# Attention, Fourier mixing and a two-layer network on one core: norm statistics spread over engines, two-part queries and keys in quarter-array form, eleven plain tiles

## The chip, the cores and the metric

One core of one Trainium2 chip. The metric is device time in microseconds of one execution, the median over several runs. The engines are TensorE (PE; its weight loads are listed as PEld), VectorE (DVE), ScalarE (ACT), GpSimd (POOL) and SyncE (SP), which here issues nearly all DMA transfers from one queue.

## The reference, cut to what matters

```python
# q, k, v: (8, 8, 576, 64); window of 64 keys, causal
scores = q @ k.T / 8; scores = where(0 <= pos_q - pos_k < 64, scores, -1e9)
attn = exp(scores - max); attn = attn / (sum(attn) + 1e-9)
x = (attn @ v) as (8, 576, 512)
mixed = real(fft(fft(x, axis=1), axis=2))
u = x + mixed
un = (u - mean(u)) / sqrt(var(u) + 1e-6)        # over the 512 features
out = u + relu(un @ w1) @ w2                     # w1: 512 x 2048, w2: 2048 x 512
```

All in float32. Most products are made in two 16-bit parts, high and low: a float32 value is split as hi = f16(x), lo = f16(x - hi), and a product needs three passes (hi hi, hi lo, lo hi; the list `PASSES`).

## The kernel before, in words

The 8 x 576 rows are 36 tiles of 128 rows. A tile T of a pair of batches goes through `attn_tile`; nine tiles are a pair. After tiles 4 and 8 of a pair the Fourier block `fft` of one batch follows, and then `norm_tile` for the four or five tiles that are complete. Two tiles make a chunk of 256 rows for the two layers: `ffn(0)` in float32 ("plain"), `ffn` of chunks 1 to 13 in two parts, `ffn7` of chunks 14 to 17 with a scheme of seven products. The weights come as 32 pieces of 512 KB, converted on VectorE in three steps (`weight_piece`), squared on ScalarE for their size, and split into two parts once all are there.

**Attention.** Tiles 0 to 12 (`whole`, T < PRO = 13) are plain: queries, keys and the weights of attention are turned with TensorE transposes in float32, and the score uses quarters of the array, 64 rows by 64 columns (L662). From tile 13 on all is in two parts: keys and queries are split (ScalarE or VectorE for the high, GpSimd or VectorE for the low part), turned with DMA transposes, one for the keys and two for the queries, which are laid out doubled (`qpad`, `qbd`). The keys stand as 128 rows, 64 of high and 64 of low parts, so that one matmul of 128 rows makes two of the three passes (L667); the score of a tile is two operations, one for the even and one for the odd heads (`score((g,))`). Behind the score come the mask with the row maximum (VectorE), the exponential (ScalarE), the turning of the weights, the product with the values (`av`, L746), and `normed` on VectorE: add 1e-9 to the sum, reciprocal, multiply (L752 to L758). Then a radix-4 step, whose result is turned on TensorE if `soon` (plain tiles, and tiles 4 and 8 of a pair), else by transfer.

**Norm.** `norm_tile`: for tiles from 2 on a gather (GpSimd's queue) brings the mixed rows; `stats` on VectorE adds them to x, takes `bn_stats` and `bn_aggr` and adds 1e-6 (L1092 to L1105); `rstd` on GpSimd raises to the power -0.5 (L1109); `scale` on VectorE makes un (L1113). Then un is split and turned for the chunk.

**Order.** Every piece of work is an `op` with an engine, or two to choose from (`alt`). The order in which all ops of all engines are issued is a list of numbers in the file (`ORDER`), and `SECOND` holds those that go to their second engine. `Plan.follow` walks the list; where its own arithmetic sees a gap on TensorE of over 0.8 us before the first layer begins, the kernel puts filler matmuls (`warm`, L1625). Each engine does its instructions in the order of the list; an op waits for its inputs by semaphores. All loads, transposes and stores stand in SP's queue in the order of the list.

Of the kernel before, what the change touches and what calls it, by code (L numbers as in the profile page):

```python
# [12 lines left out]
F32 = mybir.dt.float32  # L13
F16 = mybir.dt.float16
# [4 lines left out]
AF = mybir.ActivationFunctionType  # L19
# [27 lines left out]
PRO = 13  # L47
# [3 lines left out]
WSC = 1.1  # L51
W_DMA, W_DMA_STEP, W_CONV, W_SQ, W_SPLIT, W_STEP = -20, 1.6, 40, 60, 60, 0.5
VS = 64.0
YS = 32.0
# [138 lines left out]
""".split()}  # L193


# [1461 lines left out]
```

## Time and profile before

| | |
|---|---|
| median of 3 runs | 962.61 us (962.05 to 963.97) |
| span of the profiled execution | 961.9 us |
| outside the span, against the median | 0.7 us (no other time of that execution is given) |
| TensorE busy | 941.0 us, 98% |
| VectorE, ScalarE, GpSimd busy | 748.8, 413.2, 326.8 us |
| mean granted clock of TensorE | 0.995 |

A busy TensorE includes matmuls that overlap each other and filler; its time is best read from the starts of successive groups. Rows below are named Rows 1 to Rows 9. "L667" is line 667 of the kernel, "psc" the score's tile, "pa" the product with the values, "ph" and "po" the first and second layer's, "pk", "pq", "pp", "py" the results of transposes.

### The profile page before, as it was taken

What the parts mean: (1) busy time and instruction counts of PE and PEld (TensorE: products, weight loads), DVE (VectorE), ACT (ScalarE), POOL (GpSimd) and SP (SyncE); (2) the same over time, 40 slices, a digit from 0 to 9 for tenths busy, and PEclk for the clock granted to TensorE, in tenths of its full rate; (3) what the DMA queues carried; (4) which work ended last, traced back from release to release, by engine and by line L of the source; (5) the groups of instructions that cost most, each with busy time, mean ns of one, the idle gap of its engine ahead of it and who ended that gap; (6) DMA issues with size and microseconds to landing.
All of it is one profiled execution on the core that took longest, in us unless ns stands there. A gap on an engine that the chain in (4) does not pass through costs nothing.

```text
span 961.9 us, 23560 instructions
## 1 busy us (share of the span) xinstructions
PE 941.0 (98%) x9251; PEld 700.8 (73%) x9251; DVE 748.8 (78%) x2038; ACT 413.2 (43%) x929; POOL 326.8 (34%) x616
## 2 busy tenths in 40 slices
PE   7899999999999999999999999999999999999998
PEld 5677677676776676667676677667676668888887
DVE  6899788887887778786766877786887999686654
ACT  7775667734633344333533235333443334222231
POOL 1543333134643342413421424223333422241231
PEclk9999999999999999999999999999999999999999
DMA  9886735336797748697768665676765301121000
GB/s 220 228 253 188 214 88 136 75 92 127 137 206 175 158 93 166 154 176 149 139 140 170 127 127 97 153 139 154 118 151 91 81 13 34 38 54 46 23 33 23
DMA packets 307294, 119.93 MB, mean 125 GB/s; under 512 B 290728, under 2 KB 291112, under 8 KB 307184
## 3 DMA queue, kind: packets, MB, share of 16 engines
q1 hardware_dynamic: 304320, 109.40, 52.9%
q0 software_dynamic: 2720, 8.92, 3.6%
q8 instruction: 72, 1.18, 0.5%
q14 instruction: 38, 0.31, 0.1%
q10 hardware_dynamic: 144, 0.13, 0.0%
HBM read 54.99 MB, written 14.17 MB: 72 GB/s over the span
## 4 chain that ended last, share of the span: by engine, by line
PE 84%; DVE 8%; DMA 4%; issue 1%; POOL 1%; ACT 1%; SPq 0%; DVEq 0%; POOLq 0%; ACTq 0%
PE ph L1297 27%; PE po L1278 27%; PE ph L1451 9%; PE po L1426 7%; PE pa L746 3%; PE pz L1011 3%; PE pg L977 2%; PE psc L667 2%; DMA kn<-in_k 1%; DVE td L1371 1%; PE pp L703 1%; DMA kst<-flex 1%; PE py L837 1%; PE psc L662 1%; PE warm L1625 1%
## 5 line engine op out<-in xcount | busy, mean ns | idle before, releaser
L1278 PE MATMUL po<-w1s,hh 128*128 128x512 f16 (+1 forms) x1312 | 332.0, 390 | 1.4 <-DVE xu L1332 1.4
L1297 PE MATMUL ph<-uhl,w0s 128*128 128x256 f16 (+1 forms) x2616 | 330.6, 278 | 2.0 <-DVE hh L1309 1.7
L1297 PEld LDWEIGHTS <-w0s 128*128 128x128 f16 x2496 | 242.7, 98 | 62.9 <-issue 3.5
L1278 PEld LDWEIGHTS <-hh 128*128 128x128 f16 x1248 | 119.7, 98 | 106.9 <-issue 1.6
L1306 ACT ACTIVATE hh<-ph 128x512 f16<-128x512 f32 x104 | 61.9, 596 | 185.9 <-PE ph L1297 135.5
L692 ACT ACTIVATE pr<-pr,nm 128x128 f32<-128x128 f32 x288 | 91.3, 391 | 25.3 <-DVE nm L684 25.1
L1309 DVE SCALAR_TENSOR_TENSOR hh<-ph,hh 128x512 f16<-128x512 f32 x104 | 71.3, 685 | 30.1 <-ACT hh L1306 29.6
L1451 PE MATMUL ph<-uhl,w0s 128*128 128x256 f16 x768 | 90.6, 273 | 0.0
L1451 PEld LDWEIGHTS <-w0s 128*128 128x128 f16 x768 | 75.1, 98 | 9.6
L496 POOL TENSOR_TENSOR flex<-pr,flex 128x128 f16<-128x128 f32 x72 | 36.6, 539 | 111.8 <-ACT flex L486 67.7
L1085 POOL DMA_INDIRECT mt<-md,gix x34 | 36.2, 1065 | 104.3 <-DVE xu L1100 44.9
L684 DVE CUSTOM_DVE_ANT_0 pr<-psc,mskb 128x128 f32<-128x128 f32 x288 | 65.0, 284 | 8.0 <-PE psc L667 5.9
L1109 POOL TENSOR_TENSOR rs<-mv,mhalf 128x1 f32<-128x1 f32 x36 | 25.5, 709 | 104.4 <-DVE mv L1105 104.1
L496 POOL TENSOR_TENSOR up<-un,up 128x128 f16<-128x128 f32 x64 | 32.1, 531 | 53.7 <-ACT up L486 37.6
L1467 DVE TENSOR_TENSOR hx<-hx 128x128 f32<-128x128 f32 x100 | 26.1, 304 | 29.5 <-ACT hx L1462 28.7
L1462 ACT ACTIVATE hx<-ph 128x512 f32<-128x512 f32 x31 | 18.3, 597 | 71.5 <-PE ph L1451 62.3
L1426 PEld LDWEIGHTS <-hh 128*128 128x128 f16 x434 | 42.4, 98 | 4.8
L746 PE MATMUL pa<-ve,pt 128*64 128x65 f16 (+1 forms) x760 | 41.2, 205 | 2.8 <-ACT pt L486 1.3
L746 PE MATMUL pa<-va,pt 128*64 128x65 f16 (+1 forms) x760 | 41.3, 205 | 0.0
L496 POOL TENSOR_TENSOR flex<-kn,flex 128x128 f16<-128x128 f32 x52 | 27.0, 550 | 30.9 <-ACT flex L486 30.9
L1475 DVE TENSOR_TENSOR hl<-hx,hh 128x896 f16<-128x896 f32 x27 | 29.6, 1106 | 9.0 <-ACT hh L486 8.3
L496 POOL TENSOR_TENSOR flex<-qn,flex 128x128 f16<-128x128 f32 x72 | 32.0, 479 | 9.1 <-ACT flex L486 8.9
(221 smaller groups left out, 1610.2 us busy)
## 6 DMA issues: line engine op xcount, KB each, us to landing
wd<-in_moe_w_ch SPq DMA_DIRECT2D x20, 512.0 KB, 5.1
out<-xu SPq DMA_DIRECT2D x35, 256.0 KB, 2.7
kn<-in_k SPq DMA_DIRECT2D x32, 256.0 KB, 3.8
qn<-in_q SPq DMA_DIRECT2D x32, 256.0 KB, 4.2
flex<-in_moe_w_ch SPq DMA_DIRECT2D x12, 512.0 KB, 3.4
ve<-va SPq DMA_DIRECT2D x43, 130.0 KB, 2.5
flex<-in_v SPq DMA_DIRECT2D x20, 256.0 KB, 3.6
md<-mp SPq DMA_DIRECT2D x24, 192.0 KB, 2.3
```

Source lines behind the costliest of these rows:

```text
L496: eng.tensor_tensor(out=out[:, k : k + w], in0=in0[:, k : k + w], in1=in1[:, k : k + w], op=al)
L684: nc.vector.tensor_tensor_reduce(out=t["pr", g][:, hp], in0=t["ps", g][:, hp], in1=mskb[:, m : m + P], scale=-0.125, scalar=3.0e38, op0=AL ...
L692: nc.scalar.activation(pr, pr, AF.Exp, bias=t["nm", g][:, hp : hp + 1], scale=-1.0)
L746: nc.tensor.matmul(pa[sl, hp], pt[:, sl], v_, start=(x == 0), stop=(x == len(mm) - 1))
L1085: nc.gpsimd.indirect_dma_start(out=mts[T], out_offset=None, in_=mds[pb][0 : HR if n < 4 else 2 * HR], in_offset=bass.IndirectOffsetOnAxis( ...
L1278: nc.tensor.matmul(t["po"][i], l_, r_, start=(f == 0 and x == 0), stop=(f == NKF - 1 and x == len(mm) - 1))
L1297: nc.tensor.matmul(ph, l_, r_, start=(x == 0), stop=(x == len(mm) - 1))
L1306: nc.scalar.activation(t["hh", j][:, 0], ph, AF.Relu)
L1309: nc.vector.scalar_tensor_tensor(out=hh[:, 1], in0=ph, scalar=0.0, in1=hh[:, 0], op0=ALU.max, op1=ALU.subtract)
L1426: nc.tensor.matmul(t["po", bk][:, x], t["h", j][a][:, slot], right(n, j, b_), start=(j == 0 and k == 0 and n in opens), stop=(j == seven - ...
L1451: nc.tensor.matmul(ph, l_, r_, start=(x == 0), stop=(x == len(mm) - 1))
L1475: eng.tensor_tensor(out=lo[:, a:b_], in0=x[:, a + 1 : b_ + 1], in1=hi[:, a:b_], op=ALU.subtract)
```

## The change

Constants: PRO 13 to 11 (tiles 11 and 12 are done in two parts), new `PSC = 1.0`, `MEANS = 2`, `CEN = 512**-0.5`. ORDER and SECOND are new throughout (3201 ops instead of 3019). The order arithmetic no longer counts the small GpSimd steps (`port=None`) as sharing a port with VectorE.

Two-part keys and queries are both split into rows [high of all heads, low of all heads] and turned by one transfer each; the score is one operation for both halves of the heads, 3 passes x 16 matmuls of 64 rows by 64 columns. `normed` becomes three ops: `guard` (ScalarE or VectorE), `inverse` (a power on GpSimd or a reciprocal on VectorE), and the multiplication. In `norm_tile`, tiles 0 and 1 keep their statistics on VectorE; for the others the sum is made by the instruction that adds, the squares on ScalarE, the root on GpSimd, and the scaling on ScalarE or VectorE. The list SECOND sends to VectorE 34 of 72 guards, 29 of 72 inverses, and 10 of 34 scalings.

```diff
-PRO = 13
+PRO = 11
+MEANS = 2
...
-            op("ACT", 0.52, base, k_hi, [bk], [bkp], alt=("DVE", 0.34, lazy))
-            op("POOL", 1.12, base + 0.1, k_lo, [bk], [bkp], alt=("DVE", 0.6, lazy))
-            op("DMA", TURN, base + 0.2, k_turn, [bkp], [bkT], lat=2.0)
-            op("ACT", 0.95, base + 0.5, lambda e: q_part(0, e), [bq], Bfl[4:6], alt=("DVE", 0.6, lazy))
-            op("POOL", 2.1, base + 0.6, lambda e: q_part(1, e), [bq], Bfl[4:6], alt=("DVE", 1.13, lazy))
-            for j in range(2):
-                op("DMA", TURN, base + 0.7, lambda j=j: q_turn(j), Bfl[4:6], [Bq[i]], lat=2.8)
+            for nm, slot, dst, bsrc, bdst, lat, at in (
+                ("kn", 0, kst_, bk, bkT, 2.0, base), ("qn", 4 + i, q16[i], bq, Bq[i], 2.2, base + 0.5)
+            ):
...
+                op("ACT", 0.52, at, hi_, [bsrc], [Bfl[slot]], alt=("DVE", 0.34, lazy))
+                op("POOL", 1.12, at + 0.1, lo_, [bsrc], [Bfl[slot]], alt=("DVE", 0.6, lazy))
+                op("DMA", TURN, at + 0.2, turn_, [Bfl[slot]], [bdst], lat=lat)
...
             for hp in range(4):
-                for z in range(1 if whole else 2):
+                for x, (a, b_) in enumerate(mm):
                     for g in groups:
+                        rows = slice(64 * g, 64 * g + 64)
                         for jj in range(2):
...
+                            nc.tensor.matmul(
+                                t["ps", g][64 * jj : 64 * jj + 64, hp], qT[rows, 4 * a + hp, 64 * jj : 64 * jj + 64],
+                                keys(4 * b_ + hp, jj, rows), start=(x == 0), stop=(x == len(mm) - 1),
+                            )
...
-            op("DVE", 0.75, base + 6.2 + 0.5 * g, normed, [bpa], [bx], port=False)
+            op("ACT", 0.1, base + 6.05 + 0.5 * g, guard, [bpa, Bmh], [brc], alt=("DVE", 0.05, 0.0), port=False)
+            op("POOL", 0.54, base + 6.1 + 0.5 * g, inverse, [Bmh], [brc], alt=("DVE", 0.08, 0.0), port=None)
+            op("DVE", 0.42, base + 6.2 + 0.5 * g, normed, [bpa, brc], [bx], port=False)
...
-            bst_ = sm.tile([P, 6], F32, tag="st", name=f"st{T}")
-            nc.vector.bn_stats(out=bst_, in_=xt)
-            t["mv"] = sm.tile([P, 2], F32, tag="mv", name=f"mv{T}")
-            nc.vector.bn_aggr(out=t["mv"], in_=bst_)
-            nc.vector.tensor_scalar(out=t["mv"][:, 1:2], in0=t["mv"][:, 1:2], scalar1=1e-6, scalar2=None, op0=ALU.add)
+                nc.vector.tensor_tensor_reduce(
+                    out=xs, in0=xs, in1=ms, scale=1.0, scalar=0.0, op0=ALU.add, op1=ALU.add, accum_out=t["sm"][sl]
+                )
...
+        def spread():
+            t["un"] = sb([P, DM], F32, "un", f"un{T}")
+            nc.scalar.activation(
+                t["un"], xts[T], AF.Square, bias=t["mv"][:, 0:1], scale=CEN, accum_out=t["mv"][:, 1:2]
+            )
...
+            nc.gpsimd.tensor_scalar(out=t["rs"], in0=t["mv"][:, 1:2], scalar1=1e-6, scalar2=None, op0=ALU.add)
+            nc.gpsimd.tensor_tensor(out=t["rs"], in0=t["rs"], in1=mhalf, op=ALU.pow)
...
+            op("DVE", sum(0.95 if r else 0.8 for _, _, r in RANGES[n]), base + 0.5, stats, [bmt], [bx, bst])
+            op("ACT", 0.72, base + 0.55, spread, [bx, bst], [bun, bst])
+            op("POOL", 1.1, base + 0.6, rstd, [bst, Bmh], [brs], port=None)
+            op("DVE", 0.05, base + 0.65, shift, [brs, bst], [bnb])
+            op("ACT", 0.62, base + 0.7, scale, [bx, brs, bnb], [bun], alt=("DVE", 0.46))
```

## Rows read from the trace of the kernel before

**Rows 1.** The page, part 1: busy us (share of the span) xinstructions.
```profile
PE 941.0 (98%) x9251; PEld 700.8 (73%) x9251; DVE 748.8 (78%) x2038; ACT 413.2 (43%) x929; POOL 326.8 (34%) x616
```

**Rows 2.** Busy time by stretch: its us, PE busy, granted clock, DMA share, GB/s.
```profile
0.00:78.00 78.00, 65.39 (x839) 0.96 0.87 227
...
125.00:400.00 275.00, 275.00 (x2699) 1.00 0.64 132
400.00:600.00 200.00, 197.41 (x2012) 1.00 0.73 142
...
700.00:800.00 100.00, 98.51 (x884) 1.00 0.37 79
```

**Rows 3.** TensorE's waits: line <- releaser: us in total, times, longest us.
```profile
PE ph L1297 <- DVE hh L1309: 1.7, 3, 0.8
...
PE po L1278 <- DVE xu L1332: 1.4, 1, 1.4
```

**Rows 4.** The chain of waits, 0 to 80 us: start us, us, what.
```profile
45.62 0.45 PE pk L553 x4
46.09 5.55 DMA qn<-in_q
...
54.26 1.69 PE pg L977 x24
...
78.02 1.99 PE ph L1297 x8
```

**Rows 5.** The timeline of TensorE, 165 to 224 us: start us, us, group.
```profile
190.44 1.10 PE L662 MATMUL psc<-kst,qbd 64*64 64x128 f32 x32
...
199.92 0.60 PE L703 MATMUL pp<-ident,pr 128*128 128x128 f32 x4
200.36 1.46 PE L1278 MATMUL po<-w1s,hh 128*128 128x512 f16 x6
```

**Rows 6.** The timeline of TensorE, 191.4 to 192.3 us.
```profile
191.48 0.27 PE L746 MATMUL pa<-ve,pt 128*64 128x65 f32 x1
...
192.10 0.39 PE L1278 MATMUL po<-w1s,hh 128*128 128x512 f16 x1
```

**Rows 7.** The timeline of TensorE, 225 to 262 us.
```profile
230.59 1.47 PE L1297 MATMUL ph<-uhl,w0s 128*128 128x256 f16 x12
231.90 1.46 PE L1278 MATMUL po<-w1s,hh 128*128 128x512 f16 x6
233.20 1.47 PE L1297 MATMUL ph<-uhl,w0s 128*128 128x256 f16 x12
...
240.22 0.62 PE L667 MATMUL psc<-kst,qbd 128*64 128x128 f16 x16
240.67 0.19 PE L746 MATMUL pa<-ve,pt 128*64 128x65 f16 x1
...
241.04 0.61 PE L667 MATMUL psc<-kst,qbd 128*64 128x128 f16 x16
241.59 2.79 PE L1297 MATMUL ph<-uhl,w0s 128*128 128x256 f16 x24
...
252.24 1.46 PE L1278 MATMUL po<-w1s,hh 128*128 128x512 f16 x6
253.63 0.64 PE L667 MATMUL psc<-kst,qbd 128*64 128x128 f16 x16
```

**Rows 8.** The chain of waits over the whole span.
```profile
84.34 1.73 PE ph L1297 x8
```

**Rows 9.** Groups by line and shape: busy us, mean ns of one, idle before.
```profile
L1102 DVE BATCH_NORM_STATS2 st<-xu 128x6 f32<-128x512 f32 x36 | 25.0, 694 | 1.2
...
L1198 DVE SCALAR_TENSOR_TENSOR w0s<-wd,w0s 128x512 uint16<-128x512 uint32 x10 | 7.9, 787 | 0.0
...
L1204 ACT ACTIVATE junk<-w1s 128x512 f32<-128x512 f32 x16 | 10.0, 626 | 1.0 <-DVE w1s L1198 1.0
...
L1109 POOL TENSOR_TENSOR rs<-mv,mhalf 128x1 f32<-128x1 f32 x36 | 25.5, 709 | 104.4 <-DVE mv L1105 104.1
```

More of the change, by code (lines that the diff above doesn't have):

```diff
@@ L352, in follow @@
                 st = max(st, done[d.idx] + after + late * self.LATE[d.eng])
-            shared = e == "POOL" or e == "DVE" and o.port
+            shared = e == "POOL" and o.port is not None or e == "DVE" and o.port
             if shared:
@@ L409, in attn_fft_ffn_kernel @@
     mhalf = cp.tile([P, 1], F32, name="mhalf")
+    mone = cp.tile([P, 4], F32, name="mone")
+    eps = cp.tile([P, 2], F32, name="eps")
     mskb = cp.tile([P, 3 * P], BF16, name="mskb")
@@ L447, in attn_fft_ffn_kernel @@
     op("POOL", 0.3, -500, lambda: make_identity(nc, ident), writes=[Bid])
-    op("POOL", 0.1, -499, lambda: nc.gpsimd.memset(mhalf, -0.5), writes=[Bmh])
+    small = ((mhalf, -0.5), (mone, -1.0), (eps[:, 0:1], 1e-9), (eps[:, 1:2], VS * 1e-9))
+    op("POOL", 0.4, -499, lambda: [nc.gpsimd.memset(a_, v_) for a_, v_ in small], writes=[Bmh])
     op("POOL", 0.3, -300, lambda: nc.gpsimd.memset(unit, 1.0), writes=[Bones])
@@ L533, in attn_tile, with keys @@
         kst_ = (kst32 if whole else kst16)[:, T % 3 * kw : (T % 3 + 1) * kw].rearrange("p (h s) -> p h s", s=P)
-        def keys(h, jj, rows=slice(None)):
+        def keys(h, jj, rows):
             if jj or n == 0:
@@ L676, in attn_tile @@
             bpt.append([bt])
-            if not whole:
-                op("PE", 0.52, base + 2 + g, lambda g=g: score((g,)), rd, [bs, bp])
             def masked(g=g):
@@ L746, in av, with guard, inverse @@
                             nc.tensor.matmul(pa[sl, hp], pt[:, sl], v_, start=(x == 0), stop=(x == len(mm) - 1))
+            def guard(eng, g=g):
+                rc = t["rc", g] = sm.tile([P, 4], F32, tag="rc", name=f"rc{T}_{g}")
+                den = t["pa", g][:, :, 64]
+                if eng is nc.scalar:
+                    eng.activation(rc, den, AF.Identity, bias=eps[:, 0:1] if whole else eps[:, 1:2])
+                else:
+                    eng.tensor_scalar(out=rc, in0=den, scalar1=1e-9 if whole else VS * 1e-9, scalar2=None, op0=ALU.add)
+            def inverse(eng, g=g):
+                rc = t["rc", g]
+                if eng is nc.gpsimd:
+                    eng.tensor_tensor(out=rc, in0=rc, in1=mone, op=ALU.pow)
+                else:
+                    eng.reciprocal(rc, rc)
             def normed(g=g):
-                pa = t["pa", g]
                 xv = xts[T].rearrange("p (h d) -> p h d", h=H)
-                rc = sm.tile([P, 4, 1], F32, tag="rc", name=f"rc{T}_{g}")
-                nc.vector.tensor_scalar(
-                    out=rc, in0=pa[:, :, 64:65], scalar1=1e-9 if whole else VS * 1e-9, scalar2=None, op0=ALU.add
-                )
-                nc.vector.reciprocal(rc, rc)
                 nc.vector.tensor_tensor(
-                    out=xv[:, g::2], in0=pa[:, :, 0:64], in1=rc.to_broadcast([P, 4, 64]), op=ALU.mult
+                    out=xv[:, g::2], in0=t["pa", g][:, :, 0:64], in1=t["rc", g].unsqueeze(2).to_broadcast([P, 4, 64]), op=ALU.mult
                 )
@@ L1077, in norm_tile @@
         t = {}
[L1078 removed]
+        bmt, bst, brs, bnb, bun, bpu = Buf("mt") if T > 1 else Bmt[T], Buf(), Buf(), Buf(), Buf("un"), Buf("ps")
         if col == 0:
@@ L1093, in stats @@
             xt, mt = xts[T], mts[T]
+            if T < MEANS:
+                for p, m, rev in RANGES[n]:
+                    assert not rev
+                    nc.vector.tensor_tensor(out=xt[p : p + m], in0=xt[p : p + m], in1=mt[p : p + m], op=ALU.add)
+                bst_ = sm.tile([P, 6], F32, tag="st", name=f"st{T}")
+                nc.vector.bn_stats(out=bst_, in_=xt)
+                t["mv"] = sm.tile([P, 2], F32, tag="mv", name=f"mv{T}")
+                nc.vector.bn_aggr(out=t["mv"], in_=bst_)
+                return
@@ L1094, in stats @@
+            t["sm"] = sm.tile([P, 1], F32, tag="st", name=f"sm{T}")
+            t["mv"] = sm.tile([P, 2], F32, tag="mv", name=f"mv{T}")
             for p, m, rev in RANGES[n]:
-                sl = slice(p, p + m)
+                sl, first, by = slice(p, p + m), xt[p : p + m, 0:1], CEN / -DM
+                xs, ms = (xt[sl, 1:DM], mt[sl, DM - 1 : 0 : -1]) if rev else (xt[sl], mt[sl])
                 if rev:
-                    nc.vector.tensor_tensor(out=xt[sl, 1:DM], in0=xt[sl, 1:DM], in1=mt[sl, DM - 1 : 0 : -1], op=ALU.add)
-                    nc.vector.tensor_tensor(out=xt[sl, 0:1], in0=xt[sl, 0:1], in1=mt[sl, 0:1], op=ALU.add)
-                else:
-                    nc.vector.tensor_tensor(out=xt[sl], in0=xt[sl], in1=mt[sl], op=ALU.add)
@@ L1101, in stats @@
-            bst_ = sm.tile([P, 6], F32, tag="st", name=f"st{T}")
-            nc.vector.bn_stats(out=bst_, in_=xt)
-            t["mv"] = sm.tile([P, 2], F32, tag="mv", name=f"mv{T}")
-            nc.vector.bn_aggr(out=t["mv"], in_=bst_)
-            nc.vector.tensor_scalar(out=t["mv"][:, 1:2], in0=t["mv"][:, 1:2], scalar1=1e-6, scalar2=None, op0=ALU.add)
+                    nc.vector.tensor_tensor(out=first, in0=first, in1=mt[sl, 0:1], op=ALU.add)
+                nc.vector.tensor_tensor_reduce(
+                    out=xs, in0=xs, in1=ms, scale=1.0, scalar=0.0, op0=ALU.add, op1=ALU.add, accum_out=t["sm"][sl]
+                )
@@ new lines, in stats @@
+                nc.vector.tensor_scalar(
+                    out=t["mv"][sl, 0:1], in0=t["sm"][sl], scalar1=first if rev else by, scalar2=by if rev else None,
+                    op0=ALU.add if rev else ALU.mult, **({"op1": ALU.mult} if rev else {}),
+                )
[3 more added lines that the diff above has]
+                t["un"], xts[T], AF.Square, bias=t["mv"][:, 0:1], scale=CEN, accum_out=t["mv"][:, 1:2]
+            )
@@ L1113, in scale @@
             nc.vector.tensor_scalar(
-                out=t["un"], in0=xts[T], scalar1=t["mv"][:, 0:1], scalar2=t["rs"], op0=ALU.subtract, op1=ALU.mult
+                out=t["nb"], in0=t["mv"][:, 0:1], scalar1=t["rs"], scalar2=1.0 / CEN, op0=ALU.mult, op1=ALU.mult
             )
+        def scale(eng=nc.vector):
+            if T < MEANS:
+                t["un"] = sb([P, DM], F32, "un", f"un{T}")
+                nc.vector.tensor_scalar(
+                    out=t["un"], in0=xts[T], scalar1=t["mv"][:, 0:1], scalar2=t["rs"], op0=ALU.subtract, op1=ALU.mult
+                )
+            elif eng is nc.scalar:
+                nc.scalar.activation(t["un"], xts[T], AF.Identity, bias=t["nb"], scale=t["rs"])
+            else:
+                nc.vector.tensor_scalar(
+                    out=t["un"], in0=xts[T], scalar1=t["rs"], scalar2=t["nb"], op0=ALU.mult, op1=ALU.add
+                )
```

79 lines of the change are left out of this document (26 added, 53 removed), and 270 rows, old and new, of tables (ORDER, SECOND).

## The prediction

> **What bounds the kernel now.** I read the page's busy line first: TensorE is busy for 98% of the span, VectorE, the next, for far less [rows 1]. A busy TensorE can still wait or run filler, so next came its busy time by stretch [rows 2]. From 0 to 78 us it is busy for 65.4 of 78 us, a part of which is filler (the "warm" matmuls that the code puts into planned gaps); from 125 to 400 us it is busy without a gap at the full granted clock (1.00, which is the 2.4 GHz level); from 400 to 600 it lacks 2.6 us, from 700 to 800 1.5 us. The list of its waits says what the gaps are: a few single ones, the longest together 1.7 and 1.4 us, both for VectorE [rows 3]. So three quantities make the span: when chunk 0 of the feed-forward part starts (78.0 us, the end of the opening), how much TensorE work lies behind that, and a few microseconds of stalls. In the opening the chain goes through loads, tile 4, and the first Fourier block: the flip of tile 6's keys at 45.6 us, a load of tile 7's queries, the second piece of the block's first stage at 54.3 us, chunk 0 at 78.0 us [rows 4]. What VectorE, ScalarE and GpSimd save or take on counts only through those three.
>
> **Tiles 11 and 12 leave the plain form.** A plain tile costs TensorE five groups of four transposes (keys, queries, two of the weights of attention, one of y); one group takes 0.44 us, the distance of two starts [rows 5]. The score takes 191.48 - 190.44 = 1.04 us and one product with the values 192.10 - 191.48 = 0.62 us; each holds one change of array form at 0.10 us (below), so 0.94 and 0.52 [rows 5, 6]. Sum: 2.2 + 0.94 + 2 x 0.52 = 4.2 us. In two parts all five groups go (keys, queries, weights and y are turned by transfers; tiles 11 and 12 are not among those whose y is still turned on TensorE) and what is left is a score and two products, 0.67 + 2 x 0.38 = 1.43 us by the next paragraph. Two tiles: 2 x 2.77 = 5.5 us less. Both stand behind the start of chunk 0, where TensorE has next to no gaps, so that the time is on the path.
>
> **The new score.** Today a score is two operations of 16 matmuls each (128 rows, 64 columns of the array, 128 columns moved). From one to the product behind it is 0.45 us, so 0.90 us for a tile; one product of 24 matmuls takes 241.04 - 240.67 = 0.37 us [rows 7]. The new one has 48 matmuls, three passes instead of two, but each uses a quarter of the array, as the plain score does. The plain one shows nearly four at once: 32 records in the 0.94 us above are 29 ns from start to start, while a full-array record in this type needs 1.73/8 = 216 ns for 256 columns [rows 8], 108 ns for 128, that is 3.7 times 29. In the 16-bit type twelve matmuls of 256 columns take 1.31 us (230.59 to 231.90) [rows 7], 55 ns for 128 columns, a quarter of which is 14 ns. So 48 x 14 = 0.67 us, 0.23 us less for each of the 23 tiles that have two parts already: 5.3 us. The bounds: 0.64 us if nothing at all is lost between four, and 48 x 29 = 1.41 us if quarters can start no closer in this type than in the other. I take 0.67, because pairs of halves lose only that little (16 matmuls in 0.45 us are 28 ns each, half of 55).
>
> **Changes of form.** TensorE does not go from one array form to another for nothing. A second-layer operation takes 1.30 us to its successor when that is of its own form (231.90 to 233.20) and 1.39 us when a score follows (252.24 to 253.63); a score takes 0.55 us when a full-array matmul follows (241.04 to 241.59) and 0.45 us when a product does (240.22 to 240.67) [rows 7]. So 0.10 us for each change, both ways. Today scores and products share a form and stand together often. The new score has a third one, and the new order scatters it: counted along TensorE's operations of the two order lists from chunk 0 on, neighbours of different form are 95 before and 165 after. 70 x 0.096 = 6.7 us more. Bounds: 0.08 to 0.11 us a change, 5.6 to 7.7 us.
>
> **Sum on TensorE** behind the start of chunk 0: -5.5 - 5.3 + 6.7 = -4.1 us. All feed-forward matmuls are as many as before.
>
> **The work taken from VectorE** is off the path but for single waits. Away go, for 34 tiles, the statistics (0.69 us and two small steps) [rows 9] and in 24 of them the scaling; by the second-engine list 38 of 72 guards go to ScalarE and 43 of 72 inverses to GpSimd; the queries' parts are half as wide. ScalarE takes on 34 squarings, each like the weights' squaring of 0.63 us with a read of its sum behind it [rows 9], and 24 scalings of about the same size: some 40 us on an engine that is busy for 43%. GpSimd takes on 43 powers and 36 small additions, a power being 0.71 us for one column [rows 9], bounded by 0.7 and, at four columns, 2.8 us: 30 to 120 us on an engine that is busy for 34%; I take the lower end, as its fixed part should rule at so few elements. The cover is that TensorE runs ahead on ready chunks. Where the cover is gone, a tile's norm has two more steps in its chain (an addition on GpSimd, a multiplication on VectorE) with their handovers: at 0.1 to 0.7 us for each, the upper end being the power, 0.2 to 1.4 us late for each such tile. On the other side the waits for VectorE (1.7 and 1.4 us) can go [rows 3]; I take 1 us of these 3.1 as a gain, about a third, since the new table places its work anew. Queued behind the squaring on ScalarE stand the exponentials and the first layer's relu; behind the added powers on GpSimd the low halves and the gathers. So -1, between -4 and +4 us.
>
> **Transfers.** A two-part tile has one transpose less on SP's queue (one for the queries in place of two, and half their bytes); tiles 11 and 12 add five transposes and two copies each. Tile by tile the turned halves come before TensorE needs them, or the stretches of [rows 2] would not be full; the cover is the chunk in work. Priced at 0; the gaps from 400 to 800 us, 4.1 us, bound what a transfer can give back, and I keep -1 and +1.
>
> **The opening.** Both lists put nearly the same TensorE work ahead of chunk 0 (46.6 and 46.9 us by the slots above) and the same norm of tiles 0 and 1, which keeps its statistics on VectorE. What differs is the order of loads on SP's queue: the new one begins with a weight piece and interleaves them tighter; ahead of tile 6's keys stand 3 weight pieces of 512 KB and 2 input loads of 256 KB more. At 227 GB/s [rows 2] that is 2.1 MB, 9 us: that flip moves from 45.6 to about 55 us, and the first Fourier stage stands behind it. In the kernel before, its second piece ran at 54.3 us, behind a load of tile 7's queries that held the chain from 46.1 to 51.6 us [rows 4]; so of the 9 us some 3 come through there. Against that the new list has on VectorE, between tile 4's radix step and tile 0's sum, 12 steps of weight conversion instead of 19; at 0.79 us, the last of a piece's three [rows 9], that is up to 5.5 us back, of which the part counts that stood on the way to chunk 0. Between -4 and +7 us I take +1, since the loads come first and VectorE's relief only where it is waited for.
>
> **Result.** 961.9 - 4.1 - 1 + 1 = 957.8 us of span. The median of the runs is 962.6, 0.7 us more than the profiled span, for which I add the same: 958.5 us.
>
> **Rivals.**
> (a) The opening gets longer. The loads of tiles 4 to 8 land late behind weight pieces, chunk 0 starts at 85 instead of 78 us, and the gain is eaten: 961.9 + 0.7 - 4.1 - 1 + 7 = 964.5 us, slower. From 83 us on nothing of the gain is left. For it: 0.87 of the transfer time in that stretch is taken [rows 2], so that a load put forward delays another; against it: VectorE's share of the wait gets shorter.
> (b) Quarters start no closer than 29 ns in the 16-bit type [rows 5, 6]: 25 x (1.41 - 0.67) = 18.5 us, 977 us. For it only that no row shows the new form; against it: halves start 0.37/24 = 15 ns apart in the products [rows 7]. The Trainium skill, TensorEngine Tiling (Array Packing), section Instruction Overhead, states about 60 cycles for each matmul however few its columns; at 2.4 GHz my estimate from that is 25 ns, and this rival would come out at about 972 us by it. The 15 ns of the products speak against that figure.
> (c) The relief on VectorE removes the late stalls too and the early weights shorten the opening: the 2.6 and 1.5 us of gaps [rows 2] down to 1, 2.1 more than taken, and chunk 0 at 76 instead of 79: 958.5 - 2.1 - 3 = 953.4 us. For it: both named waits are VectorE's; against it: ScalarE and GpSimd, through which the norm now passes once more each, can come late in their place.
> (d) The longer norm or the powers on GpSimd come late at some ten chunks by 0.4 us each, and nothing else changes: 962.5 us, the same.
>
> **Chances.** The forecast, 955 to 960.7: 0.53. (c): 0.15. (d) and what falls between 960.7 and 964.5: 0.16. (a): 0.11. (b): 0.05. Within 0.2% is 1.9 us around 962.6, which is what a measurement can tell from no change: faster 0.68, same 0.16, slower 0.16. The range of 8 in 10 takes in (c) and the edge of (a): 952.5 to 965. The forecast's own range is 955 to 960.7.
>
> **What would show it.** In the changed profile: a two-part score of 48 records whose starts are 14 ns apart on average, 29 ns under (b); 0.10 us before and behind it; no transposes for tiles 11 and 12; the first matmul of chunk 0 at 79 us (83 or more under (a), 76 under (c)); TensorE's gaps behind that of 5 us or less (nearer 10 under (d)). The forecast is wrong in its cause, even at the right time, if chunk 0 starts more than 3 us off and stalls make it good.

## The result, and the profile after

The changed kernel takes 969.68 us (median of 10 runs, 967.56 to 978.89) beside 962.43 us (959.88 to 965.00) of the kernel before in the same session: ratio 1.0077, 95% interval 1.0054 to 1.0101. It is slower by some 7 us; the forecast was 958.5, its range of 8 in 10 was 952.5 to 965. The profile of after is that of its fastest execution, 967.56 us.

The busy lines of the page of after (busy us, share of the span, instructions) and the shares of its chain of waits by engine:

```profile
PE 941.5 (97%) x9646; PEld 688.5 (71%) x9646; DVE 688.9 (71%) x1940; ACT 427.3 (44%) x1010; POOL 455.7 (47%) x866
...
PE 74%; DMA 9%; DVE 8%; POOL 5%; issue 2%; ACT 1%; SPq 1%; DVEq 0%; POOLq 0%; ACTq 0%
```

The same shares in a second profile of the kernel before, taken with the experiments:

```profile
PE 89%; DVE 6%; DMA 3%; POOL 1%; issue 0%; ACT 0%; SPq 0%; DVEq 0%; POOLq 0%
```

VectorE is relieved by 60 us as meant [rows 1]. But the chain that sets the end left TensorE for 26% of the span where it had left it for 11% (16% in the first profile of before). GpSimd has 129 us more: 50 are powers of the denominators, 9 the norm's longer step, and the other 70 are mostly splits, radix steps and Fourier steps that the new table (the lists ORDER and SECOND) put there. VectorE's instructions take no longer for it: its step of the first layer's relu takes 686 ns in both kernels, its masks 285 (groups by shape).

TensorE's busy time by stretch in after (stretch, its us, busy us, granted clock, DMA share, GB/s), to be read beside [rows 2]:

```profile
0.00:78.00 78.00, 64.89 (x836) 1.00 0.90 230
78.00:125.00 47.00, 45.65 (x334) 1.00 0.65 192
125.00:400.00 275.00, 272.78 (x2839) 1.00 0.69 134
400.00:600.00 200.00, 198.32 (x2141) 1.00 0.68 132
600.00:700.00 100.00, 98.51 (x1020) 1.00 0.63 127
```

and the last of these stretches in before:

```profile
600.00:700.00 100.00, 100.00 (x1036) 1.00 0.68 138
```

There are now gaps from 125 to 400 us, where [rows 2] had 275 full microseconds, and from 600 to 700; from 400 to 600 less is missing than before. What TensorE waited for from 78 us on, the longest rows (line <- releaser: us in total, times, longest), in before:

```profile
PE ph L1297 <- DVE hh L1309: 1.7, 3, 0.8
PE po L1278 <- DVE xu L1332: 1.4, 1, 1.4
```

and in after:

```profile
PE ph L1330 <- DVE hh L1342: 2.4, 3, 1.0
PE po L1311 <- DVE hh L1342: 1.9, 3, 0.8
PE pa L729 <- DMA pt<-flex: 0.9, 3, 0.3
```

VectorE's two rows come to 4.3 us in after and 3.1 in before (0.9 in a second profile of before); "hh" is the first layer's relu.

The new score does what the forecast said. TensorE's timeline of after (start us, us, group):

```profile
249.53 1.46 PE L1311 MATMUL po<-w1s,hh 128*128 128x512 f16 x6
250.91 0.87 PE L652 MATMUL psc<-kst,qbd 64*64 64x128 f16 x48
251.71 0.61 PE L1311 MATMUL po<-w1s,hh 128*128 128x512 f16 x2
```

From its start to the next group are 0.80 us, 0.67 for 48 matmuls and 0.13 for the change of form; 1.38 us ahead of it, where a neighbour of the same form comes after 1.30.

**Where the time went.** Two numbers of each profile split the span: the start of chunk 0's first matmul, and what lies behind it. For clean openings on both sides (no dip of the clock, see the end) they are:

```profile
77.10 5.45 PE L1297 MATMUL ph<-uhl,w0s 128*128 128x256 f32 x24 [0.24 <-ACT uhl L486]
```

in the second profile of before (span 957.9, so 880.8 us behind it), and in after (span 965.8, so 885.4 behind):

```profile
79.14 0.63 PE L1151 MATMUL pu<-ident,un 128*128 128x128 f32 x4 [0.71 <-DVE un L1133]
...
80.44 3.72 PE L1330 MATMUL ph<-uhl,w0s 128*128 128x256 f32 x16
```

So 7.9 us = 3.3 in the opening + 4.6 behind it. The TensorE work behind it, counted operation by operation at the slots without a wait (distances of starts such as the 0.67 above, 0.096 for each change of form), is 3.8 us less, so its stalls are 8.4 us more. The two profiles that do have a dip, before's first and after's second, give 5.2 and 2.4 us for the two parts, and 6.2 of stalls; over all four pairs of profiles the stalls grow by 5.3 to 9.3 us.

### The profile page after: what moved, and what is told of

Its sections match the earlier page's. It is cut to its first block, busy times and chain, and to the rows that moved or that the text cites. A ratio compares the mean times of both kernels' runs of the same rounds, so it can differ in the third digit from the quotient of the medians.

```text
span 965.8 us, 24609 instructions
## 1 busy us (share of the span) xinstructions
PE 941.5 (97%) x9646; PEld 688.5 (71%) x9646; DVE 688.9 (71%) x1940; ACT 427.3 (44%) x1010; POOL 455.7 (47%) x866
## 4 chain that ended last, share of the span: by engine, by line
PE 74%; DMA 9%; DVE 8%; POOL 5%; issue 2%; ACT 1%; SPq 1%; DVEq 0%; POOLq 0%; ACTq 0%
PE po L1311 24%; PE ph L1330 23%; PE ph L1484 9%; PE po L1459 7%; PE pa L729 3%; PE pz L1006 2%; PE pg L972 2%; DMA py<-yp 2%; DMA uhl<-up 2%; PE psc L652 2%; DMA mt<-md,gix 2%; DVE pr L667 1%; POOL flex L508 1%; DMA qn<-in_q 1%; POOL y L508 1%
## 5 line engine op out<-in xcount | busy, mean ns | idle before, releaser
L1311 PEld LDWEIGHTS <-hh 128*128 128x128 f16 x1248 | 117.7, 98 | 107.5 <-DVE hh L1342 4.2
L742 POOL TENSOR_TENSOR rc<-rc,mone 128x4 f32<-128x4 f32 x43 | 49.7, 1158 | 104.4 <-ACT rc L735 56.6
L1080 POOL DMA_INDIRECT mt<-md,gix x34 | 40.5, 1193 | 75.9 <-DVE mv L1108 55.4
L508 POOL TENSOR_TENSOR flex<-pr,flex 128x128 f16<-128x128 f32 x92 | 45.6, 524 | 23.1 <-ACT flex L498 16.8
L1459 PEld LDWEIGHTS <-hh 128*128 128x128 f16 x434 | 42.4, 98 | 4.9
L1508 POOL TENSOR_TENSOR hl<-hx,hh 128x256 f16<-128x256 f32 (+1 forms) x40 | 25.8, 674 | 41.0 <-ACT hh L498 22.2
L508 POOL TENSOR_TENSOR up<-un,up 128x128 f16<-128x128 f32 x60 | 28.4, 502 | 31.2 <-ACT up L498 21.2
L508 POOL TENSOR_TENSOR y<-xu 128x128 f32<-128x128 f32 x76 | 37.6, 524 | 9.9 <-DVE xu L748 6.6
L1105 DVE CUSTOM_DVE_ANT_0 xu<-xu,mt 128x511 f32<-128x511 f32 (+6 forms) x50 | 35.2, 703 | 9.5 <-DMA mt<-md,gix 9.3
L1115 ACT ACTIVATE un<-xu,mv 128x512 f32<-128x512 f32 x34 | 24.4, 717 | 36.1 <-DVE mv L1108 26.7
```

The lines of the kernel that those rows point to most:

```text
L508: eng.tensor_tensor(out=out[:, k : k + w], in0=in0[:, k : k + w], in1=in1[:, k : k + w], op=al)
L742: eng.tensor_tensor(out=rc, in0=rc, in1=mone, op=ALU.pow)
L1080: nc.gpsimd.indirect_dma_start(out=mts[T], out_offset=None, in_=mds[pb][0 : HR if n < 4 else 2 * HR], in_offset=bass.IndirectOffsetOnAxis( ...
L1311: nc.tensor.matmul(t["po"][i], l_, r_, start=(f == 0 and x == 0), stop=(f == NKF - 1 and x == len(mm) - 1))
L1459: nc.tensor.matmul(t["po", bk][:, x], t["h", j][a][:, slot], right(n, j, b_), start=(j == 0 and k == 0 and n in opens), stop=(j == seven - ...
```

## Experiments

Ratios are to the kernel before, run on the same chip with each group; the last two columns come from one profile each. Two profiles of the unchanged kernel differ by 3.1 us in the last column, so that verdicts rest on the ratios and the profiles only say where. In nine of the profiles the granted clock fell for a few microseconds in the opening, so that the start of their chunk 0 contains it: before's first, after's second, the inverses on VectorE, the opening of before, the inverses on GpSimd, all three, one pass, and both paddings.

The expectations below weigh four explanations. Theory 1: the powers on GpSimd keep VectorE, and through it TensorE, waiting. Rival 1: the norm's longer chain does. Rival 2: the opening is longer. Rival 3: the new table's order does it in itself. A flip is a turn by transposes on TensorE.

| kernel | ratio | 95% interval | chunk 0 starts | behind it |
|---|---|---|---|---|
| before, first and second profile | 1 | | 78.0, 77.1 | 883.9, 880.8 |
| after, first and second profile | 1.0077 | 1.0054 to 1.0101 | 80.4, 83.2 | 885.4, 886.3 |
| after, inverses on VectorE | 1.0059 | 1.0041 to 1.0077 | 84.9 | 883.3 |
| after, old norm | 1.0157 | 1.0131 to 1.0182 | 80.4 | 893.6 |
| after, old norm, guards, inverses | 1.0208 | 1.0174 to 1.0241 | 80.7 | 900.6 |
| before, new score | 0.9996 | 0.9984 to 1.0008 | 77.6 | 881.7 |
| after, opening of before | 1.0102 | 1.0080 to 1.0124 | 85.6 | 882.5 |
| after, opening of before, chunk 0 first | 1.0073 | 1.0051 to 1.0095 | 77.4 | 891.1 |
| before, new norm | 1.0038 | 1.0022 to 1.0054 | 77.8 | 887.2 |
| before, inverses on GpSimd | 1.0186 | 1.0165 to 1.0208 | 83.3 | 894.6 |
| before, all three | 1.0173 | 1.0149 to 1.0197 | 83.2 | 895.5 |
| after, no guards and inverses | 1.0024 | 1.0007 to 1.0040 | 79.5 | 882.5 |
| after, no chain of the norm | 1.0067 | 1.0048 to 1.0086 | 80.3 | 884.6 |
| after, neither | 1.0012 | 0.9998 to 1.0027 | 78.7 | 881.4 |
| after, guards and inverses on VectorE | 1.0090 | 1.0069 to 1.0111 | 79.9 | 888.8 |
| before, one pass of the new score | 0.9897 | 0.9880 to 0.9915 | 80.7 | 871.9 |
| after, padding on VectorE | 1.0087 | 1.0065 to 1.0110 | 81.8 | 888.7 |
| after, padding on GpSimd | 1.0077 | 1.0053 to 1.0100 | 82.0 | 886.9 |

**Undoing the parts in the new order.** Inverses moved by the second-engine list (43 operations):

```
+SECOND |= {...}   # the 43 "inverse" operations that stood on GpSimd
```

> The kernel after, with all 43 inverses of the softmax's denominators that stood on GpSimd (power, 1.16 us each in its trace) made by VectorE's reciprocal; guards stay on ScalarE, everything else and the order stay. Theory 1 (GpSimd's powers, twice as long as the plan's 0.54, keep VectorE and through it TensorE waiting): most of the loss comes back, 964 to 966 us, and the stalls of TensorE behind chunk 0's start fall from 9.8 us towards 6. Rival 1 (the norm's longer chain): no change, 968 to 970. Rival 2 (the opening): at most the 2.4 us by which chunk 0 starts later, 967, and chunk 0 starts at 79 or before. Rival 3 (the new table's order itself): no change, 968 to 970.

Ratio 1.0059: 1.7 us less by the ratios, within the intervals of both. The place of the powers is a small part, though they cost what was feared; groups of after by line and shape (busy us, mean ns of one | idle before):

```profile
L742 POOL TENSOR_TENSOR rc<-rc,mone 128x4 f32<-128x4 f32 x43 | 49.7, 1158 | 104.4 <-ACT rc L735 56.6 <-DVE rc L737 45.4 <-DMA out<-xu 2.2
...
L1122 POOL TENSOR_TENSOR rs<-rs,mhalf 128x1 f32<-128x1 f32 x36 | 23.7, 658 | 3.0
...
L748 DVE TENSOR_TENSOR xu<-pa,rc 128x256 f32<-128x256 f32 x72 | 29.5, 419 | 9.6 <-POOL rc L742 8.7
```

The last row is the scaling: in all 72 together VectorE waits 8.7 us for the powers.

One place where they cost is plain in the chain of waits of after (start us, us, what):

```profile
82.04 1.49 POOL rc L742
83.53 0.19 issue
83.72 6.69 DMA mt<-md,gix
90.44 0.68 DVE xu L1105
...
93.37 0.29 DVE pr L667
...
95.14 0.35 DVE w0s L1219
95.49 1.19 PE pp L686 x4
```

GpSimd issues the gather of a norm tile behind a power; the rows land at 90.4 us; VectorE, in its order, waits for them with the sum of the norm and holds back the next tile's masked scores; TensorE's transposes of that tile come late. From 90 to 96.5 us TensorE's operations start 1.9 us later than their slots. With the inverses on VectorE the same sum starts 7.0 us behind chunk 0's start (91.94 - 84.9) instead of 10.0, and that stall is gone:

```profile
86.87 1.31 POOL L1082 DMA_INDIRECT mt<-md,gix  x1 [4.05 <-DMA flex<-in_moe_w_ch]
```

```profile
91.94 0.69 DVE L1107 CUSTOM_DVE_ANT_0 xu<-xu,mt 32x512 f32<-32x512 f32 x1 [0.70 <-DMA mt<-md,gix]
```

Not every stall starts there. The seven largest of after behind chunk 0's start, by the distances of starts in its trace, are 0.7 to 1.2 us each, 6.7 together, of which the two at 90 to 96.5 us are 1.9. Two others stand behind GpSimd's Fourier steps (timelines of after; in brackets the wait before it and its releaser). VectorE waits for a step of GpSimd, the relu of the first layer is queued behind, and TensorE waits for the relu:

```profile
685.05 0.96 DVE L508 TENSOR_TENSOR xe<-yT 128x772 f32<-128x772 f32 x1 [2.25 <-POOL yT L508]
687.33 1.47 PE L1330 MATMUL ph<-uhl,w0s 128*128 128x256 f16 x12 [0.61 <-DVE hh L1342]
...
698.10 0.71 DVE L508 TENSOR_TENSOR f<-xe 128x388 f32<-128x388 f32 x1 [2.93 <-POOL hs L508]
700.24 1.04 PE L1311 MATMUL po<-w1s,hh 128*128 128x512 f16 x4 [0.81 <-DVE hh L1342]
```

These two steps (yT from py, and hs) take 46 us on GpSimd in after and 25 in the second profile of before: they are part of the 70 us that the table moved.

Then the norm's work as before (plain sums, bn_stats, bn_aggr and the 1e-6 on VectorE; squares and shift empty), in the new order:

```
-                nc.vector.tensor_tensor_reduce(out=xs, in0=xs, in1=ms, ..., accum_out=t["sm"][sl])
+                nc.vector.tensor_tensor(out=xt[sl], in0=xt[sl], in1=mt[sl], op=ALU.add)
...
+            nc.vector.bn_stats(out=bst_, in_=xt)
...
+SECOND |= {...}   # all 34 scalings on VectorE
```

> The kernel after, with the norm's work as it was before, in the new table: plain adds, statistics and the 1e-6 on VectorE, only the power on GpSimd, every scaling on VectorE; ScalarE's squares and scalings and VectorE's shift are gone. GpSimd loses 11 us, ScalarE 44 us, VectorE gains about 23 us. Theory 1 (GpSimd's powers of the denominators): little change, 967 to 970. Rival 1 (the norm's longer chain through four handovers): 964 to 966. Rival 3 (the new table's order itself): no change or longer, 969 to 973, since this table counts on a shorter VectorE.

1.0157, 7.7 us worse than after: rival 1 falls in its plain form. VectorE is busy for 724.8 us there, still less than the 749 of before, and yet this order cannot place the work. With all guards and inverses back on VectorE too:

> The kernel after, with both undone: the norm's work as before, and all guards and inverses on VectorE as before; what is left of the change is the new form of the two-part scores, the [high, low] rows, two tiles fewer in plain form, and the new table. Theory 1 and rival 1: 959 to 963, the shorter TensorE work shows. Rival 3 (the new table's order itself, with its 165 instead of 95 changes of form): 967 or more even so. Rival 2 (opening): chunk 0 still starts at 80 or later if the table's order of loads and weights did it, at 78 if the powers did.

1.0208. By name this is what rival 3 said, but it says only that the new order does not suit the old steps, which stand in the places of the new ones and were not given an order of their own. So the parts were put into the old order.

**The parts alone in the old order.** The score (its 48 matmuls stand where the later of the two old halves stood; the second operation is empty):

```
-                                nc.tensor.matmul(out, qbd[i][:, jj, h, 64 * z : 64 * z + 64], keys(h, jj), ...)
+                                nc.tensor.matmul(t["ps", g][64 * jj : 64 * jj + 64, hp],
+                                    qT[rows, 4 * a + hp, 64 * jj : 64 * jj + 64], keys(4 * b_ + hp, jj, rows), ...)
```

> The kernel before, its table and 13 plain tiles, with only the two-part q and k in [high, low] rows, one transfer each, and the score of 48 quarters in one place (where the second half of the score stood). Theory 1, rivals 1 and 2: the form is sound, TensorE's work falls by 23 x (0.90 - 0.67) = 5.3 us less some 2 us for longer changes of form, 958.5 to 961. Rival 3 or a form that costs more than its slots show: 962.5 or more. Against it stands that the whole score now waits for the later of its two places, which may cost a few tenths at a few tiles.

0.9996: no difference that can be told. By slots TensorE has 5.1 us less of scores and 2.0 more of changes of form (116 for 95), and its stalls are 3.9 us longer than in the second profile of before, but only 0.9 longer than in the first. By the ratio some 2.7 us of the 3.1 are lost. One of the stalls is the merging itself: the score of tile 24 is cut in two by a wait for VectorE (timeline of this kernel).

```profile
460.33 0.24 PE L662 MATMUL psc<-kst,qbd 64*64 64x128 f16 x2
461.34 0.86 PE L662 MATMUL psc<-kst,qbd 64*64 64x128 f16 x46 [0.76 <-DVE xu L752]
```

The norm alone, its square and power issued at the old power's place, shift and scaling at the old scaling's:

```
         def rstd():
+            if T >= MEANS:
+                spread()
...
         def scale():
+            if T >= MEANS:
+                shift()
```

> The kernel before, its table and form, with only the norm's work as after: sum by the add, squares on ScalarE, 1e-6 and power on GpSimd, shift on VectorE, scaling on ScalarE for the 24 tiles where after has it; each new step is issued in the place of the old step that follows it. Rival 1 (the norm's longer chain costs): 964 or more. Theory 1 and rival 3 (the chain is no loss in itself, VectorE is relieved by 23 us): 960 to 963.

1.0038, 3.7 us slower: in an order that has no room for its longer chain the new norm costs, though VectorE falls from 749 to 716.6 us. The inverses on GpSimd alone, and all three parts together:

```
+                if (T, g) in POOLINV:
+                    nc.gpsimd.tensor_tensor(out=rc, in0=rc, in1=mone, op=ALU.pow)
+                else:
+                    nc.vector.reciprocal(rc, rc)
```

> The kernel before, its table and form, with the 43 inverses that after has on GpSimd made there (38 of its guards on ScalarE), issued right behind the product whose denominators they need. Theory 1 (the powers of 1.16 us keep VectorE waiting): 964 to 968. Rival 3 (the table): up to 963, the wait of VectorE is covered as the first runs suggest, where taking the powers away gave 0.7 us of 7.

> The kernel before, its table, with all three parts of the change at once, the new score and rows, the new norm and the inverses on GpSimd; only the table and the 13 plain tiles are those of before. Rival 3 (the loss of the kernel after sits in the new table's order): 960 to 963. Theory 1 or rival 1, or the three together (the parts cost in themselves): 966 or more.

1.0186 and 1.0173. Rival 3's bound of 963 is missed by far, and so is theory 1's 964 to 968: where nothing is moved to make room, 43 powers cost 17.9 us, 6 of them in the opening (chunk 0 at 83.3, in a profile with a dip of the clock). In the new order they cost far less, at most 5.1 us with all that goes with them (below). A part of the 17.9 us is TensorE's clock. In the profile with the inverses on GpSimd TensorE waits 3.74 us for the relu, and its granted clock is 0.50 (the level of 1.2 GHz) from 301 to 307 us (stretch, its us, busy us, granted clock, DMA share, GB/s):

```profile
301.93 2.72 PE L1314 MATMUL ph<-uhl,w0s 128*128 128x256 f16 x12 [3.74 <-DVE hh L1326]
```

```profile
301.00:307.00 6.00, 5.07 (x18) 0.50 0.39 89
```

On 5.07 busy us that is some 2.5 us, an estimate from this row. The mean granted clock of the five executions of that kernel is 0.994 to 0.996, beside 0.998 to 1.000 for before in the same session.

**The opening.** The 356 operations ahead of chunk 0 in the order and on the engines of before:

> The kernel after, with the 356 operations ahead of chunk 0's first matmul put in the order (loads, weights, conversions) and on the engines that they had before, guards and inverses of that stretch on VectorE; from chunk 0 on the new table stands. Rival 2 (the opening's new order costs): chunk 0 starts at 78 instead of 80.4 us and the time falls by 2.4 us or more, to 967 or below; if slower executions of the kernel after lose their time in the opening too, to 965. Rival 3 (the table behind it): time falls by less than 1 us, since what is late behind the opening stays late, 969 to 970.

1.0102, slower than both forecasts. The norm's second flip came at 77.2 us, 1.9 earlier than in after, but a tile's transposes, which the old order puts behind chunk 0's start, now stood in front of it and waited. Hence the same again, with two operations moved:

```
-... N1 flip ... T9 flip q ... T7 flip_p1 ... C0 one2 ... C0 one0 ...
+... N1 flip ... C0 one2 C0 one0 T9 flip q ... T7 flip_p1 ...
```

> As the run with the opening of before (loads, weights, conversions and engines ahead of chunk 0 as before), but chunk 0's first two products stand right behind the second flip of the norm; in the run before this one a tile's transposes stood ahead of them and waited 4.1 us. Rival 2 (the opening's new order costs 2.4 us): chunk 0 starts at 79 or before and the time falls to 965 to 967.5. Rival 3 (the order behind the opening): 969 or more, chunk 0 starts sooner but what follows it stalls by as much.

```profile
77.44 3.72 PE L1340 MATMUL ph<-uhl,w0s 128*128 128x256 f32 x16 [0.68 <-ACT uhl L508]
```

Chunk 0 starts 3.0 us earlier than in after, and the time is the same, 1.0073: chunk 1's first matmul, at 156.8 us in after, comes at 158.0. But only the first 16 of chunk 0's matmuls came sooner. The next 8 come later than in after; first after, then this kernel:

```profile
84.44 1.89 PE L1330 MATMUL ph<-uhl,w0s 128*128 128x256 f32 x8
```

```profile
85.79 1.89 PE L1340 MATMUL ph<-uhl,w0s 128*128 128x256 f32 x8
```

So the old order of loads and conversions does not bring the time back, and rival 2 is not borne out. Whether an opening that is shorter as a whole would show in the time was not tried.

**Leaving work out.** These kernels leave steps out, to see what their time is worth. Guards and inverses empty, the scaling by a constant tile; the norm's squares, power and shift empty, scaling by constants; both:

```
             def guard(eng, g=g):
+                pass
...
             def inverse(eng, g=g):
+                pass
```

> The kernel after with the softmax's guards and inverses left out on every engine (the products are scaled by a constant tile): 43 powers, 38 guards on ScalarE and 63 small VectorE steps fewer, and the two handovers between product and scaling gone. Theory 1 (the powers and their handovers make the rest late): 963 to 966. Rivals 1 and 3: 967.5 to 969.5, as with the inverses on VectorE (968.98).

> The kernel after with the norm's squares, power and shift left out for the 34 tiles of the loop (the scaling uses constants; the sum made by the add stays): ScalarE -24 us, GpSimd -33, VectorE -7, and three handovers fewer between the sum and the scaling. Rival 1 (the norm's longer chain makes TensorE wait): 963 to 966, stalls of TensorE behind chunk 0 down from 13 to 8 us. Theory 1 and rival 3: 967.5 or more.

> The two together: guards and inverses, and the norm's squares, power and shift left out. What is left over before's 962.5 is neither the powers nor the norm's chain. Theory 1 or rival 1: 960 to 963. Rival 3 (the order itself, its opening, its late transfers and flips of form): 965 or more.

1.0024, 1.0067 and 1.0012. The softmax's denominators are worth 5.1 us by the ratios (0.0053 x 962.5), the norm's chain 1.0, which its interval does not part from nothing, both together 6.3. These are upper bounds for the added steps: the kernels also leave out what before does in some form, 63 of its small VectorE steps at the denominators and the variance. With both gone the time is still 1.2 us above before's, a difference that its interval does not part from nothing, with 3.8 us less TensorE work and 4.4 us more stalls than in the second profile of before. What TensorE waits for there from 78.8 us on, the three longest rows:

```profile
PE ph L1316 <- DMA uhl<-up: 1.2, 1, 1.2
PE po L1297 <- DVE hh L1328: 1.1, 2, 0.8
PE pa L729 <- DMA pt<-flex: 0.9, 2, 0.5
```

The first and the third are DMA transposes. Of the second, 0.8 us come from a relu on VectorE that is queued behind a norm's sum, which waits for its gather:

```profile
396.92 0.69 DVE L1096 CUSTOM_DVE_ANT_0 xu<-xu,mt 96x512 f32<-96x512 f32 x1 [3.32 <-DMA mt<-md,gix]
```

**What in the denominators costs?** All guards and inverses on VectorE in the new order:

```
+SECOND |= {...}   # all 72 guards and 72 inverses
```

> The kernel after with all 72 guards and all 72 inverses on VectorE, as before has them, each in its place of the new order; ScalarE loses 38 guards, GpSimd 43 powers. If the handovers cost the 4.3 us that came back when guards and inverses were left out: 965 to 967. If the work itself does, wherever it stands, or VectorE has no room for it in this order: 968 to 971.

1.0090: not better than after. So neither GpSimd's power nor the handover is the price by itself. That these steps, on any engine, make the scaling late because the order has it planned tight is my reading of this; no run shows it directly. Then whether one engine's queue is full:

```
+                [nc.vector.memset(pad, 0.0) for _ in range(3)]   # ahead of each of the 72 scalings
```

```
+                [nc.gpsimd.memset(pad, 0.0) for _ in range(2)]   # at each of the 72 inverses
```

> The kernel after with three tiny memsets, which nobody reads, ahead of each of the 72 scalings of the softmax on VectorE, some 0.2 us each time and 14 us in all (its busy share goes from 71 to 73%). If VectorE's queue paces TensorE's stalls in the new order: 973 to 980, a third or more of the added time. If it has room: 969 to 971.

> The kernel after with two tiny memsets, which nobody reads, on GpSimd at each of the 72 places of an inverse, some 0.2 us each time and 14 us in all (its busy share goes from 47 to 49%). If GpSimd's queue paces TensorE's stalls in the new order (theory 1 in its wider form): 973 to 980. If it has room: 969 to 971.

The groups by line of the two kernels show what was added:

```profile
L749 DVE MEMSET pad<- 128x2 f32 x216 | 13.0, 60 | 7.0
```

```profile
L742 POOL MEMSET pad<- 128x2 f32 x144 | 15.2, 106 | 4.6
```

The memsets on VectorE overlap its other instructions in part, and its busy time grows by 6.2 us (688.9 to 695.1); GpSimd's grows by 14.9 (455.7 to 470.6). The ratios are 1.0087 and 1.0077, both within the interval of after. So neither queue is full at these places, and theory 1 falls in its wider form as far as these places show.

**Does TensorE's work count at all?** One of three passes of the score, in the old order:

```
-            mm = ONE if whole else PASSES
+            mm = ONE
```

> The kernel before with the new rows and score, of which only the first of its three passes is made (16 quarters for 48 in 23 tiles; the two correcting passes are left out). TensorE's work falls by 23 x 0.45 = 10.3 us below that of the run with the whole new score (962.2). If TensorE's work sets the time one for one: 952. If other engines and transfers pace a part of it: 955 to 960, the rest turned into waits of TensorE.

0.9897: by the ratios 9.5 us less than with all three passes, of 10.3 taken away. TensorE's work does reach the time nearly one for one; what the new score lost in the old order it lost, by this, in new waits and changes of form.

The second profiles of both kernels, from which numbers stand above:

> The kernel before again, for a second profile. If its first profile's dip of the granted clock between 30 and 60 us was a chance of that execution, chunk 0 starts at 76 to 78 and its span is 959 to 961.

> The kernel after again, for a second profile. If its first profile was one of its fastest executions, this one has a span of 967 to 969, with the difference in the opening (chunk 0 after 81) or in the stalls of the first 300 us.

Their spans are 957.9 and 969.5 us, each just outside its forecast; chunk 0 starts at 77.1 and 83.2, as forecast.

## Why the prediction was wrong

- **TensorE's sum** was right: -3.8 us by the same count in the changed trace, -4.1 forecast. The quarters keep their 14 ns (0.67 us), a change of form costs 0.13 us out of the score, 0.03 more than the 0.096 taken. Rival (b) is out. The Trainium skill's TensorEngine Tiling (Array Packing) states about 60 cycles for each matmul in its section Instruction Overhead, 25 ns by the prediction's estimate. The trace does not agree where four quarters run side by side: the 48 starts are 14 ns apart.
- **The work taken from VectorE** is the step that failed. It was priced at -1 us, "off the path but for single waits", with the cover that "TensorE runs ahead on ready chunks". In its place stalls grew by 8.4 us in the clean pair (5.3 to 9.3 over the four pairs). Leaving out the softmax's denominators gives 5.1 us of the time back, leaving out the norm's chain about 1. Sizes were off too: the power of four columns was taken at the lower end, 0.7 us, and measured 1.16, so that powers and additions on GpSimd took 60.8 us where 30 was the low end. But that is not the whole error, since reciprocals on VectorE in the same order win 1.7 us back by the medians. The error was to price the steps by their engines' free time. Each stands in a chain (product, guard, inverse, scaling, radix step; gather, sum, square, power, shift, scaling) whose end something waits for, on engines that work in order; the padding shows that free time was there. How the 8.4 us divide between longer chains and the order's new places stays open: the trace shows both kinds, a gather behind a power at 82 us and Fourier steps on GpSimd at 685 and 698.
- **The table was taken as neutral.** I counted its changes of form (+6.7 us, in line with the count of the work) and took 1 us of its new places as a gain. That gain rested on two waits of one execution: a second profile of before has 0.9 us of them in place of 3.1. The waits were also read too narrowly. Over the whole span the list of [rows 3] names GpSimd and loads as well, with 1.7, 1.5 and 1.4 us; only from 78 us on are VectorE's the longest. The old steps in the new order (1.0208) and the new steps in the old one (1.0173) are both far worse than either kernel: neither set of steps fits the other's order. Stalls beyond those of the two chains are left in the new order: without either it has 0.6 us more behind chunk 0's start than the second profile of before with 3.8 us less work, that is 4.4 us of stalls. What the table would have to change to be rid of these was not settled. The 70 us of other steps that the table moved to GpSimd were not tried by themselves.
- **The opening** was forecast at +1 and came out at +2.4 against the first profile, +3.3 against the clean one. The reason given, weight pieces ahead of the inputs, holds for its middle (tile 4's score starts at 35.9 us for 32.3). But the term itself, the seventh flip of keys (tile 6's, if the tiles still go in turn) at 55 us for 45.6, did not come: it stands at 46.3 us in after. Putting the loads back does not change the time.
- **Rival (d)**, a late norm or late powers at some ten chunks, named the mechanism and was undersized: 962.5 us by 0.4 us each. The seven largest stalls of after are 0.7 to 1.2 us each. Its sign came: TensorE's stalls behind chunk 0's start, by the distances of starts, are some 10 us in after.
- **Transfers** were priced at nothing; no run parts them from the rest. The chain of after passes through DMA transposes (py, uhl) and through gathers (mt) for about as long, 17 to 19 us each; in the second profile of before the gathers are 4.5 us of the chain and these two transposes do not stand in it. Shares of the span by line, from the page of after:

```profile
PE po L1311 24%; PE ph L1330 23%; PE ph L1484 9%; PE po L1459 7%; PE pa L729 3%; PE pz L1006 2%; PE pg L972 2%; DMA py<-yp 2%; DMA uhl<-up 2%; PE psc L652 2%; DMA mt<-md,gix 2%; DVE pr L667 1%; POOL flex L508 1%; DMA qn<-in_q 1%; POOL y L508 1%
```

- **The base** was an execution slower than the median. The 0.7 us put outside the span are 1.8 in the two profiles of which the execution's own time is on record (967.56 for 965.8, 959.66 for 957.9), so that the first profile of before belongs to a time of some 963.7 us, an estimate.

No complete version here beats the kernel before: the new score alone comes out level.

## What to carry to other kernels

Work that is moved off a busy engine is not free on idle ones: price a step by the chain it lengthens, and ask which in-order engine stands waiting at that chain's end and what is queued behind it. An order tuned for one set of steps is part of the price of any other set, so test an edit in both orders before crediting it. Two profiles of the same kernel can differ by as much as the effect; take a second one before explaining 3 us.

## What the runs showed of the hardware

The granted clock falls in the opening in some executions of one kernel. TensorE by stretch in the first and in the second profile of before:

```profile
30.00:60.00 30.00, 24.59 (x295) 0.89 0.90 245
```

```profile
30.00:60.00 30.00, 23.37 (x334) 1.00 0.94 248
```

and in the second profile of after:

```profile
30.00:60.00 30.00, 23.94 (x317) 0.94 0.95 236
```

These are short pieces at the lower of the two levels, 1.2 GHz. In the first profile of before:

```profile
34.00:38.00 4.00, 2.36 (x20) 1.00 0.85 212
38.00:42.00 4.00, 3.55 (x30) 0.57 0.94 278
42.00:46.00 4.00, 3.66 (x68) 1.00 0.56 133
```

TensorE was busy for 2.36 of 4 us before the clock fell, and for 3.55 of 4 before it rose. With the dip chunk 0 starts 0.9 us later in before and 2.8 in after, while the clock alone takes up to 3.3 and 1.8 us of 30 (estimates from the means of 0.89 and 0.94): the two do not go together, and the dip explains only a part of the spread of 5 us between executions of one kernel. In one session the fastest and the slowest of 17 executions of before, 960.5 and 965.8 us, both have a mean granted clock of 1.000.

A power on GpSimd took 0.66 us for one column and 1.16 for four (before, one column took 0.71 [rows 9]): a fixed part of about 0.5 us and 0.17 for each column, an estimate from these two rows. On ScalarE a square of 512 columns with a sum cost 0.72 us and 0.19 more to read the sum, a guard of four columns 0.26, in the trace of after.
